# Down products of a bilinear gated unit: seven block products in place of eight, with weight combinations made once

## The chip, the cores and the metric

One core of a Trainium2 chip runs the kernel. The metric is the device time of one execution in microseconds. Nothing in the change or in what is told below involves a second core.

The engines are named as the profile names them: PE is TensorE (PEld its weight loads), DVE is VectorE, ACT is ScalarE, POOL is GpSimd, SP is SyncE, which here only issues transfers.

## The reference

2048 tokens of 640 features pass through a conditioned block of two parts, an S4 convolution and a bilinear gated unit (F = 1536). All is float32.

```
mod = silu(c) @ w_mod                            # six rows of 640: sa, ca, ga, sb, cb, gb
h = layernorm(x) * (1 + ca) + sa
x = x + ga * s4(h)                               # long convolution by FFT, plus a skip
h = layernorm(x) * (1 + cb) + sb
x = x + gb * (((h @ w_gate) * (h @ w_up)) @ w_down)
```

## The kernel before

**Stages.** The first 518 us or so are the modulation, the S4 convolution and the head of the second layernorm; the change leaves them alone. Then comes the gated unit. Its 2048 tokens are taken in two halves, each of two blocks (T = 0 and 1) of 512 tokens; the 1536 hidden features in NF = 12 tiles of 128, the 640 features in NB = 5 tiles of 128. A half has a gate/up loop over the 12 tiles f, and then the down products of its two blocks, one block after the other.

**A product is three matmuls.** Every float32 operand is split into a rounded part `hi` and a rest `lo` (`hilo`, line 1022): ScalarE copies, VectorE subtracts. A product is then hi·hi + lo·hi + hi·lo, three matmuls that add in PSUM (`prod`, line 1055).

**Gate and up.** The two weights and the two token blocks make a 2x2 scheme with seven products in place of eight. For each tile f these are called x_1, x_2, y_1, y_2, y_3, z_1, z_2. In matmuls of 128x512: x_1, y_1 and y_2 have 6, x_2, y_3, z_1 and z_2 have 9, 54 in all. x_1 and x_2 use the plain gate weights (`split_g`); the others use sums of weights (`sums_u` on GpSimd, lines 1036 to 1039; `split_u`) and sums of tokens (`s_sums`, `s_split`). Each product has a PSUM bank of its own out of six that take turns (`pa`, line 1063). The products are put together outside TensorE: `e` is x_1 copied by ScalarE; s6 = y_1 + e; z is z_1 copied by ScalarE; s67 = y_2 + s6; s6 = z + s6; z = z + s67 (GpSimd, line 1412); then the two halves' products a·c (VectorE, line 1423) and s·z (GpSimd, line 1430) are the hidden values. There is one buffer each for s6, z and s67.

**Order.** In each tile the loop calls y_1, z_1, x_1(i+3), parts of `split_u(i+1)`, y_2, `split_g`, `sums_u(i+2)`, x_2(i+3), y_3, z_2, and in the first half `fold(f)`. Engines run their own instructions in the order in which the code issues them.

**Down.** `fold` multiplies w_down by the row gb on GpSimd (line 1507) and writes it to DRAM as `wdg`. `raw` reloads it by SyncE, two tiles at a time, and once for every one of the four token blocks; `d_prep` splits the weights and the hidden values each time. `down` (line 1463) does for each tile 4 token groups x 3 matmuls x 2 column parts of 384 and 256, and adds over all 12 tiles in six banks. `fin` adds the residual and writes the result.

Of the kernel before, what the change touches and what calls it, by code (L numbers as in the profile page):

```python
# [224 lines left out]
def tile_kernel(ctx: ExitStack, tc: tile.TileContext, I, out):  # L225
# [762 lines left out]
    LEFT = {"wga", "wgb", "wur", "xb0", "xb1", "hh1", "hl1", "a5", "a6", "a7", "a8", "a9", "wsgh", "wsgl", "e"}  # L988

    PAIRS = []  # L990
    for h in range(2):
        PAIRS += [("g", h * NF + 2 * p) for p in range(NF // 2)]
        PAIRS += [("d", 2 * h + T, 2 * p) for T in range(2) for p in range(NF // 2)]

    def raw():

        k = PAIRS.pop(0)
        t = mk("wga", [P, 2 * D], F32, 2)
        f = k[-1] % NF
# [25 lines left out]

    def split_g(i):
        WS[i] = mk("wsgh", [P, NB, P], F32R, 4), mk("wsgl", [P, NB, P], F32R, 4)
        hilo(*WS[i], WR.pop(("g", i)))
        if i > 3:
            used(i)  # L1030

# [23 lines left out]
    def prod(ps, ks):  # L1055

        for n, (a, b) in enumerate(((0, 0), (1, 0), (0, 1))):
            for m, (w, k, x, l) in enumerate(ks):
                PE.matmul(ps, w[a][:, k], x[b][:, l], start=n == 0 and m == 0, stop=n == 2 and m == len(ks) - 1)  # L1059

    BANK = [0]

    def pa(j=None):

        if j is None:
            j = BANK[0]
            BANK[0] += 1
        return ps_a.tile([P, 512], F32, name=f"pa{j % 6}")
# [5 lines left out]
    def x_c(i):  # L1074
        V.tensor_tensor(a_tile(i % NF), UX.pop(i), UE[i], op=OP.add)

    def x_1(i):
        UX[i] = pa()
        prod(UX[i], [(WS[i], k, HX[0], k) for k in (0, 1)])
        x_e(i)  # L1080

    def x_2(i, c=True):
        UX[i] = pa()
# [17 lines left out]
    def head_st(tb):  # L1101
        if tb == 1:
            return a_tile(TV0 + NB - 1)[:, : 24 * NB].rearrange("p (i k s) -> p i k s", i=4, k=NB)
        return wp.tile([P, 4, NB, 6], F32, name="st0")
# [547 lines left out]
```

## Time and profile before

| | |
|---|---|
| runs | 1006.97, 1004.3, 1001.61 us; median 1004.3 |
| profiled execution | 1001.29 us; its span 999.2 us; mean granted TensorE clock 0.961 |
| busy, of the span | PE 900.0 us, DVE 762.8, POOL 564.3, ACT 561.9 |
| gated unit, first half | gate/up loop to about 674 us, down to 756 us |
| gated unit, second half | gate/up loop from 761 to 910 us, down to 995 us |

The profile is one execution. The sections of its page give each engine's busy time, groups of equal instructions with their mean length, the chain of work that ended last, and the transfers. A window of the trace gives the same for a stretch of time. An engine's idle time matters only where another engine, or the end, waits for it.

### The profile page before, as it was taken

To read this page: it belongs to the slowest core of one execution; us is meant where nothing else is said; L and a number is where in the kernel's file an instruction comes from. 1 tells how busy PE (TensorE), PEld (TensorE's weight loads), DVE (VectorE), ACT (ScalarE), POOL (GpSimd) and SP (SyncE) were. 2 spreads that over 40 slices of the span, in tenths; PEclk is the share of its full clock that TensorE was granted. 3 is DMA by queue.
4 is the path that set the end of the run, shared out by engine and by line. 5 is a ranking of instruction groups with operands and counts; after the bars stand their busy time and mean duration, and the time that the engine had idled before them with its cause. 6 is when DMAs were issued, how large, how long until landed. Compare 5 with 4: busy or idle time off the path is not lost.

```text
span 999.2 us, 26832 instructions
## 1 busy us (share of the span) xinstructions
PE 900.0 (90%) x11192; PEld 727.2 (73%) x11192; DVE 762.8 (76%) x1399; ACT 561.9 (56%) x1048; POOL 564.3 (56%) x415
## 2 busy tenths in 40 slices
PE   4867898899789689998888999999999999999998
PEld 3565556675576467776555888879998888889998
DVE  8798569889979997975769788777576887768452
ACT  4869989987878979752354323235463422223331
POOL 5978899799789899930032667650112365542000
PEclk9877889999899899999999999999999999999999
DMA  8728754555256454577673442535635232212341
GB/s 265 254 50 301 227 176 135 194 163 167 68 163 202 129 161 120 164 248 214 210 210 123 153 150 87 184 132 159 209 134 202 88 105 80 79 53 59 100 159 53
DMA packets 147817, 153.16 MB, mean 153 GB/s; under 512 B 9200, under 2 KB 125424, under 8 KB 146288
## 3 DMA queue, kind: packets, MB, share of 16 engines
q1 hardware_dynamic: 145968, 148.43, 46.8%
q10 hardware_dynamic: 1728, 3.02, 0.8%
q8 instruction: 88, 1.44, 0.6%
q14 instruction: 33, 0.27, 0.1%
HBM read 110.45 MB, written 40.96 MB: 152 GB/s over the span
## 4 chain that ended last, share of the span: by engine, by line
PE 63%; DVE 16%; ACT 10%; issue 4%; DMA 4%; POOL 2%; SPq 1%; DVEq 0%; ACTq 0%; POOLq 0%
PE pa L1059 26%; PE pa L1463 16%; PE kg L807 2%; DMA xsb<-A_u 2%; PE kg L822 2%; PE psfc L889 2%; ACT L230 1%; PE psfb L889 1%; PE psfa L889 1%; PE psfc L946 1%; PE psfb L946 1%; PE psfa L946 1%; PE psfc L868 1%; ACT trb L230 1%; PE psfa L844 1%
## 5 line engine op out<-in xcount | busy, mean ns | idle before, releaser
L710 POOL TENSOR_TENSOR EQ<-LQ,RH 128x1536 f32<-128x1536 f32 x40 | 124.2, 3105 | 9.9 <-DVE QtB L767 9.7
L230 ACT ACTIVATE z<-pa 128x512 f32<-128x512 f32 x24 | 14.4, 598 | 175.7 <-POOL a L1430 112.1
L1024 DVE TENSOR_TENSOR wsgl<-wga,wsgh 128x640 fp32r<-128x640 f32 x72 | 70.0, 976 | 46.1 <-ACT wsgh L230 46.1
L1412 POOL TENSOR_TENSOR z<-z,s 128x512 f32<-128x512 f32 x24 | 32.1, 1337 | 126.5 <-DVE s L1411 72.0
L230 ACT ACTIVATE wsgh<-wga 128x640 fp32r<-128x640 f32 x72 | 52.5, 732 | 65.1 <-PE pa L1463 47.9
L1024 DVE TENSOR_TENSOR wtl<-tf,wth 128x256 fp32r<-128x256 f32 (+1 forms) x72 | 42.7, 594 | 48.3 <-ACT wth L230 48.3
L1463 PE MATMUL pa<-wsgh,sh 128*128 128x384 f32 (+1 forms) x304 | 69.4, 309 | 0.0
L1463 PE MATMUL pa<-wsgh,sl 128*128 128x384 f32 (+1 forms) x304 | 69.0, 308 | 0.0
L1463 PE MATMUL pa<-wsgl,sh 128*128 128x384 f32 (+1 forms) x304 | 69.0, 308 | 0.0
L710 POOL TENSOR_TENSOR Phb<-LH,DH 128x1536 int32<-128x1536 int32 x20 | 62.3, 3115 | 11.2 <-ACT tra L230 11.2
L710 POOL TENSOR_TENSOR EP<-LP,RH 128x768 f32<-128x768 f32 x40 | 66.1, 1651 | 0.0
L710 POOL TENSOR_TENSOR Pha<-LH,DH 128x1536 int32<-128x1536 int32 (+1 forms) x21 | 62.5, 2974 | 2.2 <-ACT trb L230 1.9
L1036 POOL TENSOR_TENSOR tf<-wur,wgb 128x256 f32<-128x256 f32 x23 | 17.8, 776 | 75.6 <-DVE wtl L1024 50.0
L822 PE MATMUL kg<-QtB,PtB 64*32 64x64 f32 x2560 | 48.7, 229 | 5.4 <-DVE QtB L766 5.3
L822 PEld LDWEIGHTS kg<-QtB,PtB 64*32 64x32 f32 x2560 | 41.6, 114 | 15.4 <-issue 6.5
L1463 PEld LDWEIGHTS pa<-wsgh,sl 128*128 128x128 f32 x304 | 46.4, 187 | 0.0
L1463 PEld LDWEIGHTS pa<-wsgl,sh 128*128 128x128 f32 x304 | 46.3, 187 | 0.0
L1059 PE MATMUL pa<-sh,wtl 128*128 128x512 f32 x144 | 45.0, 394 | 1.4 <-DVE wtl L1024 1.2
L1463 PEld LDWEIGHTS pa<-wsgh,sh 128*128 128x128 f32 x304 | 46.3, 187 | 0.0
L1059 PE MATMUL pa<-sh,wth 128*128 128x512 f32 x144 | 44.9, 393 | 0.5 <-ACT wth L230 0.5
L1059 PE MATMUL pa<-sl,wth 128*128 128x512 f32 x144 | 44.5, 390 | 0.0
L1430 POOL TENSOR_TENSOR a<-s,z 128x512 f32<-128x512 f32 x24 | 38.8, 1618 | 5.4 <-DVE s L1429 5.4
(604 smaller groups left out, 2925.2 us busy)
## 6 DMA issues: line engine op xcount, KB each, us to landing
wga<-wdg SPq DMA_DIRECT2D x24, 640.0 KB, 5.0
wga<-B_w_gate SPq DMA_DIRECT2D x12, 640.0 KB, 5.9
wgb<-B_w_gate SPq DMA_DIRECT2D x24, 320.0 KB, 3.4
wur<-B_w_up SPq DMA_DIRECT2D x24, 320.0 KB, 4.0
xb<-x2d SPq DMA_DIRECT2D x6, 1280.0 KB, 5.7
TVb<-WD SPq DMA_DIRECT2D x22, 256.0 KB, 3.6
t_tw<-w_mod SPq DMA_DIRECT2D x3, 1600.0 KB, 8.5
t_ti<-w_mod SPq DMA_DIRECT2D x3, 1600.0 KB, 7.9
```

The source lines that it names most:

```text
L230: return S.activation(o, i, f, **kw)
L710: G.tensor_tensor(o.rearrange("p x (h l) -> p x h l", l=8), lo.unsqueeze(2).to_broadcast([P, rows, nh, 8]), hi.rearrange("p h x -> p x h") ...
L807: PE.matmul(kg[j * 32 : j * 32 + 32, dd, :], PtA[:, c, dl * 4 + j, :], QtA[:, c, dl * 4 + j, :], start=dd == 0 and c == 0, stop=False, til ...
L822: PE.matmul(kg[j * 32 : j * 32 + 32, dd, :], PtB[lo : lo + 64, c, r, :], QtB[lo : lo + 64, c, r, :], start=False, stop=dd == 7 and c == 1, ...
L889: PE.matmul(r[c][par * 64 : par * 64 + 64, i, :], t_tw[:, k0 + k, c, :], src[:, k, :], start=True, stop=True, tile_position=(0, par * 64))
L946: PE.matmul(r[par][:, i], t_ti[lo : lo + 64, qd * 4 + i, c, :], x[lo : lo + 64, c, i, :], start=c == 0, stop=c == 1, tile_position=(lo, 0))
L1024: V.tensor_tensor(lo, v, hi, op=OP.subtract)
L1036: E.tensor_tensor(t[:, 0:2], u[:, 0:2], g[:, 0:2], op=OP.subtract)
L1059: PE.matmul(ps, w[a][:, k], x[b][:, l], start=n == 0 and m == 0, stop=n == 2 and m == len(ks) - 1)
L1412: G.tensor_tensor(ZT[i], ZT[i], S67[i], op=OP.add)
L1430: G.tensor_tensor(a_tile(NF + i % NF), c, ZT.pop(i), op=OP.mult)
L1463: PE.matmul(ACC[tb][t][c], x[:, ts], w[:, cs], start=st, stop=f == NF - 1 and n == 2 and (c == 0 or t % 2 == 1))
```

## The change

**Down.** A half's down product is seen as a 2x2 block product: two token blocks, two halves of the hidden features (NH = 6 tiles each), two halves of 320 output columns. Seven block products j = 0 to 6 give it. `down(half, m)` is tile c of product j, m = 6j + c, with 12 matmuls of 320 columns. The sums over j stay in PSUM in two sets of four banks, "A" and "C"; `post` adds them to the residual after each product. The sums of hidden values are made by `d_sum` on GpSimd, from the end of the gate/up loop to m = 14.

**Weights.** In the first half's loop `f_load` fetches four tiles of w_down, `f_sums` multiplies them by gb and forms the combinations on GpSimd, and `f_put` splits the seven of them and writes both parts to DRAM (`wdc`). The three rounds are placed by a table over slots, three slots a tile. `w_load` brings 640 KB of these split weights by a transfer that GpSimd issues and that casts to the matmul's type, one for every two m. The split gate weights are kept in DRAM too (`wsd`), and the second half reloads them in the same way.

**Gate and up.** x_1, y_1, y_2 and y_3 of a tile now add in one bank, z_1 and z_2 in another. s67 is gone; s6 is a copy by ScalarE (for the first two tiles, whose x_1 comes earlier, still an addition by VectorE, with z + e and the last product on GpSimd). The product a·c moves from VectorE to GpSimd, the other from GpSimd to VectorE.

```
     def split_g(i):
-        WS[i] = mk("wsgh", [P, NB, P], F32R, 4), mk("wsgl", [P, NB, P], F32R, 4)
+        t = wsg()
+        WS[i] = tuple(t[:, j].rearrange("p (k m) -> p k m", k=NB) for j in range(2))
+        if i >= NF:
+            G.dma_start(t, wsd[:, i - NF])
+            return
         hilo(*WS[i], WR.pop(("g", i)))
...
     def x_1(i):
-        UX[i] = pa()
-        prod(UX[i], [(WS[i], k, HX[0], k) for k in (0, 1)])
+        UX[i] = UA[i] = pa(i % 4)
+        prod(UX[i], [(WS[i], k, HX[0], k) for k in (0, 1)], last=False)
         x_e(i)
...
     def y_1(i):
-        ps = pa()
-        prod(ps, [(WT[i], 2 + k, HX[2], 2 + k) for k in range(2)])
+        if i < 2:
+            UA[i] = pa(i)
+        prod(UA[i], [(WT[i], 2 + k, HX[2], 2 + k) for k in range(2)], i < 2, False)
         S6[i] = tmp("s6")
-        V.tensor_tensor(S6[i], ps, UE[i], op=OP.add)
+        if i < 2:
+            V.tensor_tensor(S6[i], UA[i], UE[i], op=OP.add)
+        else:
+            act(S6[i], UA[i])
 
     def z_1(i):
...
+        if i < 2:
+            G.tensor_tensor(ZT[i], ZT[i], UE[i], op=OP.add)
 
     def y_2(i):
-        ps = pa()
-        prod(ps, [(WT[i], 4 + k, HX[2], 4 + k) for k in range(2)])
-        S67[i] = tmp("s67")
-        V.tensor_tensor(S67[i], ps, S6[i], op=OP.add)
-        V.tensor_tensor(S6[i], ZT[i], S6[i], op=OP.add)
-        G.tensor_tensor(ZT[i], ZT[i], S67[i], op=OP.add)
+        prod(UA[i], [(WT[i], 4 + k, HX[2], 4 + k) for k in range(2)], False, False)
+        V.tensor_tensor(ZT[i], UA[i], ZT[i], op=OP.add)
 
     def z_2(i):
...
-        V.tensor_tensor(a, a, c, op=OP.mult)
+        G.tensor_tensor(a, a, c, op=OP.mult)
 
     def y_3(i):
...
+        if i < 2:
+            V.tensor_tensor(UE[i], UA.pop(i), UE[i], op=OP.add)
+            G.tensor_tensor(h, UE.pop(i), ZT.pop(i), op=OP.mult)
+        else:
+            V.tensor_tensor(h, UA.pop(i), ZT.pop(i), op=OP.mult)
...
+    def d_prep(m):
+        j, c = divmod(m, NH)
+        v = S1[c] if j == 3 else AT[(0, NH, 0, 0, NF, NH, NF + NH)[j] + c]
+        AH[m] = d_pair(m)
+        hilo(*AH[m], v)
...
+    def d_sum(j, c, E=G):
+        a, b = AT[c], AT[NF + c]
+        if j == 0:
...
+            E.tensor_tensor(S1[c], b, AT[NF + NH + c], op=OP.add)
+            E.tensor_tensor(b, a, b, op=OP.subtract)
+        elif j == 1:
+            E.tensor_tensor(a, S1[c], a, op=OP.subtract)
+        else:
+            E.tensor_tensor(AT[NH + c], AT[NH + c], a, op=OP.subtract)
+
+    def w_load(q):
+        WD[q] = wsg()
+        G.dma_start(WD[q], wdc[:, q // 3, q % 3])
+
+    def down(half, m, last=False):
...
+        w = [WD[m // 2][:, l, c % 2 * DC : c % 2 * DC + DC] for l in range(2)]
+        for t in range(4) if not last else (last - 1,):
+            for n, (a, b) in enumerate(((0, 0), (1, 0), (0, 1))):
+                PE.matmul(ps[t][:, :DC], AH[m][a][:, t * P : t * P + P], w[b], ...)
...
+    def post(half, j, ts=range(4), E=None):
...
+        for t in ts:
+            V.tensor_tensor(x[:, t], ps[t][:, :DC], x[:, t], op=OP.add)
...
+    def f_sums():
+        for k in range(4):
+            G.tensor_tensor(FT["f"][:, k], FT["f"][:, k], gbr, op=OP.mult)
...
+        G.tensor_tensor(t[:, 1], b22, b12, op=OP.subtract)
+        G.tensor_tensor(b12, b12, b11, op=OP.subtract)
+        G.tensor_tensor(t[:, 0], b22, b12, op=OP.subtract)
+        G.tensor_tensor(t[:, 2], b21, t[:, 0], op=OP.subtract)
+
+    def f_put(r, j, n):
...
+        act(k(hi), v)
+        V.tensor_tensor(v.bitcast(F32R), v, k(hi), op=OP.subtract)
+        SY.dma_start(wdc[:, j, r, 0], hi.bitcast(F32))
+        SY.dma_start(k(wdc[:, j, r, 1]), v)
...
+    FOLD[2] = [(f_sums,)]
+    FOLD[10], FOLD[13] = [(f_load, 1)], [(f_sums,)]
+    FOLD[21], FOLD[24] = [(f_load, 2)], [(f_sums,)]
+    for r, b in enumerate((4, 15, 26)):
+        for j in range(7):
+            FOLD[b + j] = [(f_put, r, j, r + j), *FOLD[b + j]]
...
         for f in range(NF):
             i = i0 + f
+            late = 0 < f <= NF - AHEAD
             y_1(i)
-            z_1(i)
-            late = 0 < f <= NF - AHEAD
             if late:
                 x_1(i + AHEAD - 1)
+            z_1(i)
+            fold(half, 3 * f)
...
-            y_3(i)
-            z_2(i)
-            if half == 0:
-                fold(f)
+            z_2(i)
+            fold(half, 3 * f + 1)
+            y_3(i)
+            fold(half, 3 * f + 2)
...
+        for m in range(7 * NH):
...
+            if todo and m > 0:
+                d_sum(*todo.pop(0))
+            if m % 2 == 0 and m and m // 2 + 3 < 21:
+                w_load(m // 2 + 3)
...
+                down(half, m)
+            if c == 0 and j:
+                post(half, j - 1)
```

How the change moves instructions is seen on three places. The first is GpSimd in the first half's loop, from the z of tile 0 to the z of tile 1. In the rows the name and line stand first, then what is written, what is read, and the shape; `tf` are sums of gate and up weights, `a_...` hidden values, `xb_...` the tiles of w_down. Before:

```order
L1412 TENSOR_TENSOR z<-z,s_7816 128x512
L1036 TENSOR_TENSOR tf<-wur,wgb 128x256
L1037 TENSOR_TENSOR tf<-wur,tf 128x256
L1038 TENSOR_TENSOR tf<-wur 128x256
L1039 TENSOR_TENSOR tf<-wgb,tf 128x256
L1430 TENSOR_TENSOR a_7852<-s_7816,z 128x512
L1412 TENSOR_TENSOR z<-z,s_7911 128x512
```

The same place after, from line 1437 of tile 0, which is a·c, on to the z of tile 1 (line 1423):

```order
L1437 TENSOR_TENSOR a_7630<-a_7630,s_7791 128x512
L1444 TENSOR_TENSOR a_7862<-e,z 128x512
L1546 TENSOR_TENSOR xb_7780<-xb_7780,gbr 128x640 x4
L1550 TENSOR_TENSOR xb_7781<-xb_7780 128x640
L1551 TENSOR_TENSOR xb_7780<-xb_7780 128x2x320
L1552 TENSOR_TENSOR xb_7781<-xb_7780 128x640
L1553 TENSOR_TENSOR xb_7781<-xb_7780,xb_7781 128x640
L1423 TENSOR_TENSOR z<-z,e 128x512
```

The four sums `tf` still stand ahead of line 1437; the eight operations of `f_sums` are new between the two tiles.

The second place is TensorE in tile 0 of the first half: y_1, z_1 and y_2 before, each writing a bank of its own (`pa_7782`, `pa_7791`, `pa_7809`).

```order
L1059 MATMUL pa_7782<-sh,wth 128x512 x2
L1059 MATMUL pa_7782<-sh,wtl 128x512 x2
L1059 MATMUL pa_7782<-sl,wth 128x512 x2
L1059 MATMUL pa_7791<-sh,wth 128x512 x2
L1059 MATMUL pa_7791<-hh_7624,wsuh 128x512
L1059 MATMUL pa_7791<-sh,wtl 128x512 x2
L1059 MATMUL pa_7791<-hh_7624,wsul 128x512
L1059 MATMUL pa_7791<-sl,wth 128x512 x2
L1059 MATMUL pa_7791<-hl_7625,wsuh 128x512
L1059 MATMUL pa_7809<-sh,wth 128x512 x2
```

After, in the same place:

```order
L1063 MATMUL pa_7784<-sh,wth 128x512 x2
L1063 MATMUL pa_7784<-sh,wtl 128x512 x2
L1063 MATMUL pa_7784<-sl,wth 128x512 x2
L1063 MATMUL pa_7793<-sh,wth 128x512 x2
L1063 MATMUL pa_7793<-hh_7620,wsuh 128x512
L1063 MATMUL pa_7793<-sh,wtl 128x512 x2
L1063 MATMUL pa_7793<-hh_7620,wsul 128x512
L1063 MATMUL pa_7793<-sl,wth 128x512 x2
L1063 MATMUL pa_7793<-hl_7621,wsuh 128x512
L1063 MATMUL pa_7784<-sh,wth 128x512 x2
```

The matmuls keep their order; y_2 now writes y_1's bank again.

The third place is GpSimd at the start of the first half's down products. Before, it had the end of the loop and weight sums of the next half:

```order
L1412 TENSOR_TENSOR z<-z,s_8915 128x512
L1430 TENSOR_TENSOR a_7647<-s_8915,z 128x512
L1036 TENSOR_TENSOR tf<-wur,wgb 128x256
L1037 TENSOR_TENSOR tf<-wur,tf 128x256
L1038 TENSOR_TENSOR tf<-wur 128x256
```

After, it has these (line 1489 is `w_load`, lines 1480 to 1483 are `d_sum`):

```order
L1489 DMA wsg<-wdc 128x1280 x2
L1480 TENSOR_TENSOR hh_8826<-a_8308,a_7642 128x512
L1481 TENSOR_TENSOR a_8308<-a_7634,a_8308 128x512
L1480 TENSOR_TENSOR hst<-a_8416,a_7643 128x512
L1481 TENSOR_TENSOR a_8416<-a_8060,a_8416 128x512
L1489 DMA wsg<-wdc 128x1280
L1483 TENSOR_TENSOR a_7630<-hh_8826,a_7630 128x512
L1483 TENSOR_TENSOR a_7631<-hh_8826,a_7631 128x512
L1489 DMA wsg<-wdc 128x1280
L1483 TENSOR_TENSOR a_7632<-hh_8826,a_7632 128x512
L1483 TENSOR_TENSOR a_7633<-hh_8826,a_7633 128x512
L1489 DMA wsg<-wdc 128x1280
```

Between the loads stand the sums of hidden values, two for each load, up to m = 14; the loads then follow one another with nothing between them.

288 lines of the change are left out of this document (155 added, 133 removed).

## The prediction, made before the result was known

> **What bounds the kernel now.** I read the page first, for who is busy; then the busy time in windows cut at the stages of the gated unit; then the chain of waits over that stretch; then single timelines at the places that the change touches. The page:
>
> ```profile
> span 999.2 us, 26832 instructions
> PE 900.0 (90%) x11192; PEld 727.2 (73%) x11192; DVE 762.8 (76%) x1399; ACT 561.9 (56%) x1048; POOL 564.3 (56%) x415
> ```
>
> The execution took 1001.29 us, so 2.1 us lie around the span. It is 3.0 us below the median of the runs, 1004.3; I make the sum on 1001.3 and add 3 at the end. Everything before about 518 us is left alone. The rest in windows (us, then busy time of each engine, the granted clock, the DMA share and rate):
>
> ```profile
> 520.00:545.00 25.00, 22.23 (x91) 15.15 (x90) 22.32 (x40) 14.93 (x30) 1.35 (x1) 1.00 0.37 124
> 545.00:664.00 119.00, 118.89 (x519) 96.87 (x518) 95.20 (x133) 33.17 (x77) 82.61 (x73) 1.00 0.42 138
> 664.00:675.00 11.00, 9.46 (x52) 8.13 (x51) 8.97 (x13) 4.78 (x8) 3.19 (x3) 1.00 0.49 179
> 675.00:756.00 81.00, 80.96 (x562) 80.72 (x561) 56.51 (x129) 43.24 (x70) 12.06 (x11) 1.00 0.50 163
> 756.00:761.00 5.00, 3.79 (x27) 3.53 (x25) 4.36 (x5) 2.97 (x5) 3.01 (x2) 1.00 0.00 0
> 761.00:910.00 149.00, 148.66 (x648) 121.45 (x649) 110.18 (x166) 46.08 (x102) 66.83 (x63) 1.00 0.31 98
> 910.00:995.00 85.00, 84.98 (x578) 84.57 (x576) 40.39 (x62) 27.03 (x44) 1.64 (x2) 1.00 0.31 97
> 995.00:1000.00 5.00, 0.00 (x0) 0.00 (x0) 1.22 (x3) 0.00 (x0) 0.00 (x0) 0.92 0.55 198
> ```
>
> In order these are: the start of the first half's gate/up loop, the loop, its end, the first half's down products, the turn to the second half, its gate/up, its down products, the last writes. TensorE is busy for 99.9% of the long windows at a granted clock of 1.00. Only 2.8 us are idle at the start, 1.5 us at 664:675 and 1.2 us at 756:761. So fewer matmul columns are worth their full time, and any new wait of TensorE costs its full time: there is nothing left to hide behind. The chain says the same, and prices a matmul:
>
> ```profile
> 674.50 41.92 PE pa L1463 x284
> 761.34 149.04 PE pa L1059 x648
> 910.38 84.62 PE pa L1463 x576
> 995.02 0.42 DVE xb L1478
> ```
>
> Line 1463 is the down product: 84.62/576 = 146.9 ns for a mean width of 320 columns. Line 1059 is gate/up: 149.04/648 = 230 ns for 512 columns.
>
> **The gain.** Down had 4 token blocks x 12 f x 24 = 1152 matmuls of 384 and 256 columns, 169.2 us. Seven block products of 6 f-tiles for eight leave 2 halves x 42 x 12 = 1008 matmuls of 320 columns. At the same 146.9 ns a pair of uneven ones becomes two even ones: 148.1 us. Gain 21.1 us. Gate/up keeps its 1296 matmuls. All else can only take from this.
>
> **A: the start of the first loop, +15.** The products x_1, y_1, y_2, y_3 of a tile now add into one bank, and tiles 0 and 1 have VectorE read that bank between them. The matmul rows are the start of y_2(0), of y_1(1) and of x_1(4), by the order of instructions; the last row is VectorE's read of y_1(0). A row begins with its start and length in us.
>
> ```profile
> 532.32 0.62 PE L1059 MATMUL pa<-sh,wth 128*128 128x512 f32 x2
> 540.14 0.74 PE L1059 MATMUL pa<-sh,wth 128*128 128x512 f32 x2 [0.51 <-ACT wth L230]
> 545.56 0.63 PE L1059 MATMUL pa<-hh,wsgh 128*128 128x512 f32 x2
> 540.23 0.69 DVE L1398 TENSOR_TENSOR s<-pa,e 128x512 f32<-128x512 f32 x1
> ```
>
> (a) Before, y_2(0) ran 8 us ahead of that read, in a bank of its own. Now it waits for the read, which ends at 540.9; what stands ahead of the read on VectorE has not changed. Then y_2, z_2 and y_3 are 24 matmuls, 5.5 us, so y_1(1) starts at 546.4 and not 540.14: +6.3. Before, the 15 matmuls from 540.14 to 545.56 were 3.45 us of work in 5.4, held by split weights that came late; at 546.4 these are there, so 1.9 us are won back: +4.4.
>
> (b) Before, nothing but short sums stood on GpSimd between tile 0 and tile 1. Now the first f_sums stands there, 8 operations of 128x640, ahead of z+e(1). The first row is h(0); the groups below it have busy us and mean ns of one, then the idle time before them:
>
> ```profile
> 548.80 1.75 POOL L1430 TENSOR_TENSOR a<-s,z 128x512 f32<-128x512 f32 x1
> L1507 POOL TENSOR_TENSOR xb<-xb,gbr 128x640 f32<-128x640 f32 x12 | 18.8, 1588 | 0.0
> L1374 POOL TENSOR_TENSOR a<-a,a 128x512 f32<-128x512 f32 x2 | 2.6, 1302 | 14.5 <-ACT a L230 14.5
> ```
>
> The product h(0) ended at 550.6 and should end near 551 again (its add on VectorE comes at about 547, and GpSimd has the four sums and a new a*c product ahead). Then 8 x 1.588 = 12.7 us, z+e(1) 1.3 us: 565. VectorE's add of y_2(1) needs z+e(1), and y_3(1) must not overwrite the shared bank before that add: 566. TensorE reaches y_3(1) after 45 matmuls from 546.4, at 556.8. So +9 us of idle TensorE. (c) VectorE's list, held in that add, is then behind, and x_1(5) needs what it splits: +2. Sum 15.4, taken as 15. Ends: 9, if f_sums overlaps with less (8 operations at the 1.3 us row save 2.3, and the 4.4 may partly be won back because GpSimd's loss counts from a later tile start), and 18.
>
> **B: f_sums 2 and 3 and f_put, +9.** Two more f_sums stand in tiles 4 and 8.
>
> ```profile
> 556.41 0.75 POOL L1036 TENSOR_TENSOR tf<-wur,wgb 128x256 f32<-128x256 f32 x1 [1.10 <-DVE wtl L1024]
> 557.23 1.21 POOL L1037 TENSOR_TENSOR tf<-wur,tf 128x256 f32<-128x256 f32 x1
> 558.40 0.74 POOL L1038 TENSOR_TENSOR tf<-wur 128x256 f32<-128x256 f32 x1
> 559.11 0.73 POOL L1039 TENSOR_TENSOR tf<-wgb,tf 128x256 f32<-128x256 f32 x1
> L230 ACT ACTIVATE wsgh<-wga 128x640 fp32r<-128x640 f32 x72 | 52.5, 732 | 65.1 <-PE pa L1463 47.9
> L1024 DVE TENSOR_TENSOR wsgl<-wga,wsgh 128x640 fp32r<-128x640 f32 x68 | 67.0, 986 | 46.1 <-ACT wsgh L230 46.1
> xb<-B_w_down SPq DMA_DIRECT2D x2, 1280.0 KB, 9.0
> ```
>
> In steady state a tile is 54 x 0.230 = 12.4 us of TensorE; GpSimd has 1.6 us of product and 3.4 us of sums in it, so 12.7 us of f_sums leave it 5 us late. What it is late with is a*c, which frees the one s6 buffer; ScalarE's next copy of y_1 into s6 waits, and the bank with it. With x_1, z_1 and the rest between I take 2.5 us for the second, and 5 for the third (its 1.3 MB of weights are asked for one tile, 12.4 us, earlier, and behind the last f_put, whose buffer they take; their landing alone is 9.0 us; and the last tiles have no x products to cover). f_put adds 21 ScalarE and 21 VectorE passes of 640 (0.73 and 0.99 us) to the loop; VectorE loses two adds a tile and a product, so the net is small, but they stand ahead of adds that free banks: +1.5. Bounds 0 (all absorbed in GpSimd's 7 us of slack a tile) and 17.
>
> **C: the down stages, +10.** No weight is split there any more, but GpSimd must, for every two block steps (24 matmuls, 3.53 us), form two sums and issue one casting transfer of 640 KB:
>
> ```profile
> L1024 DVE TENSOR_TENSOR wsul<-wur,wsuh 128x384 fp32r<-128x384 f32 x24 | 37.4, 1558 | 0.0
> L1024 DVE TENSOR_TENSOR wtl<-tf,wth 128x512 fp32r<-128x512 f32 x24 | 16.3, 680 | 0.0
> wga<-wdg SPq DMA_DIRECT2D x24, 640.0 KB, 5.0
> 533.93 0.37 SPq L1018 DMA_DIRECT2D wgb<-B_w_gate  x1
> ```
>
> The two sums are 2 x 1.302 = 2.6 us. VectorE's subtractions, two of 0.68 us in the same 3.53 us, read SBUF twice, and the first row shows what such an instruction suffers beside GpSimd: 384 columns take 1558 ns where 512 take 680. I charge GpSimd 1.2 us for them. Issuing a transfer from GpSimd is in no row of this trace; the nearest row is an issue of SyncE, 0.37 us, and I take 0.5. Together 4.3 us against 3.53, until the sums run out after the fourteenth step: 0.8 us lost for each of seven pairs, with the loads (5.0 us to landing) issued behind the sums, the third needed 7 us into the stage and landing at about 8.5. +5 a half. Ends 1.5 (no loss from VectorE) and 9 (2 us of issue).
>
> The Trainium skill, "SBUF — State Buffer", section "Who interferes with whom", says that a VectorE instruction with two SBUF inputs contends with a GpSimd instruction that reads SBUF, because the second input comes through the shared read interface. The 1558 against 680 ns agree. Without that rule C would be 1.5 us a half, so the sum would be 7 us lower. The Trainium skill, "DMA: Bandwidth & Descriptors", section "Anatomy of one DMA — SWDGE (gpsimd) path", fits 2.0 us plus bytes/436e3 to such a transfer: an estimate of 3.5 us for 640 KB, which would take about 1 us off C in each half. No run here shows it.
>
> **Nothing.** The turn to the second half, its loop (no f_sums, gate weights reloaded ready split) and the tail: 0, within 1. They add as many waits as they remove: the 1.2 us at 756:761 stays, the last writes still follow the last matmul by 4 us.
>
> **Sum.** 1001.3 - 21.1 + 15 + 9 + 10 = 1014.2, and 3 to the median: 1017 us. Ends: 1001.3 - 21.1 + 9 + 0 + 3 = 992 (995) and + 18 + 17 + 18 = 1033 (1036).
>
> **Rivals.** *R1, faster, 997 us.* GpSimd catches up after tile 1. For it: in 545:664 it is idle 31%, and it loses a multiplication a tile. Then A 10, B 1, C 3: 994, and 997 at the median. It decides when the waits stay under 16 us; against it, (a) and (b) rest on order alone and make 13 by themselves. Chance 0.18. *R2, no change, 1006 us.* A 15, but the bursts are mostly absorbed, B 4, C 4: 1003. Chance 0.16. *R3, much slower, 1069 us.* The casting transfer itself paces the down stage: the nearest row, 5.0 us for 640 KB, is more than 3.53; were they one after another, 42 x 5.0 = 210 us against 148: +62 in place of C's 10, 1066. Against it: the 5.0 us are a latency, and the DMA share is 0.50 in 675:756. It decides as soon as one load costs more than 3.53 us of the queue. Chance 0.09. My forecast, 1017 (own range 1009 to 1036), keeps 0.57.
>
> **Chances.** A measurement of this kernel can tell 0.5%, 5 us. Faster by more: R1, 0.18. Within: R2, 0.16. Slower: 0.57 + 0.09 = 0.66. The range leaves out most of R3 (0.07) and the lower half of R1 (0.09): 995 to 1040.
>
> **What would show it.** In the changed kernel's trace: y_1(1) starts near 546; TensorE idles for some 9 us between 556 and 566 with line 1423 on GpSimd late behind lines 1546 to 1553; smaller holes in tiles 4 and 8 to 9; holes before matmuls of line 1502 released by the transfers of wsg, in the first 14 steps of each half; the matmuls themselves at 147 ns. Wrong if a matmul of 320 columns costs other than 147 ns, if the first loop takes no longer than before, or if the transfers hold TensorE to the end of a down stage.

## The result, and the profile after

The changed kernel takes 1042.4 us (median of four runs, 1038.4 to 1043.6) against 1004.2 us before: a ratio of 1.037, 95% interval 1.033 to 1.041. The forecast was slower, at 1017 us; the measured time lies above the range (995 to 1040). The profiled execution took 1043.28 us with a span of 1041.5 us.

The page of the changed kernel, its span, busy times and transfers from GpSimd:

```profile
span 1041.5 us, 26772 instructions
PE 899.6 (86%) x11048; PEld 721.1 (69%) x11048; DVE 728.8 (70%) x1352; ACT 571.3 (55%) x1069; POOL 647.5 (62%) x509
wsg<-wdc POOLq DMA_DIRECT2D x42, 640.0 KB, 4.4
```

TensorE has 144 matmuls less and is no less busy. To see where, I divided both traces at the same events: the first y_1 matmul, and the first and last down matmul of each half. The columns are the window, its length, busy time of PE, PEld, DVE, ACT and POOL, the granted clock, DMA share and rate. First before, in the order first loop, first down stage, turn and second loop, second down stage:

```profile
527.80:668.40 140.60, 137.72 (x590) 109.45 (x590) 115.44 (x166) 45.24 (x102) 84.59 (x74) 1.00 0.43 142
668.40:759.80 91.40, 89.81 (x617) 88.75 (x615) 64.83 (x138) 48.75 (x80) 17.30 (x15) 1.00 0.46 153
759.80:910.20 150.40, 148.86 (x648) 121.63 (x649) 111.38 (x167) 46.27 (x102) 67.36 (x64) 1.00 0.31 97
910.20:995.00 84.80, 84.78 (x577) 84.39 (x575) 40.39 (x62) 26.83 (x44) 1.44 (x2) 1.00 0.31 98
```

Then the changed kernel:

```profile
533.70:711.20 177.50, 145.73 (x588) 115.09 (x589) 101.83 (x155) 64.70 (x133) 110.16 (x88) 0.91 0.63 211
711.20:801.10 89.90, 81.73 (x539) 80.70 (x538) 69.66 (x142) 37.84 (x66) 43.18 (x49) 0.96 0.77 237
801.10:954.50 153.40, 150.49 (x656) 123.19 (x655) 68.90 (x121) 51.03 (x110) 64.88 (x74) 0.99 0.36 103
954.50:1037.90 83.40, 76.77 (x505) 73.93 (x503) 58.49 (x71) 22.45 (x38) 35.34 (x38) 1.00 0.65 196
```

The first loop is 37 us longer, with 32 us of idle TensorE and a clock of 0.91. The down stages are 1.5 us shorter each, not 10.5. The turn costs 3 us. The lead up to the first y_1, 533.7 against 527.8, does the same work in both; over the kernels below that leave it alone it came out between 526 and 534, so kernels are compared by their stages.

Two places show what happens. In the first down stage, VectorE (first six rows) and GpSimd (last three), each with start and length:

```profile
712.02 1.30 DVE L1013 TENSOR_TENSOR hl<-a,hl 128x512 fp32r<-128x512 f32 x1
713.25 5.80 DVE L1013 TENSOR_TENSOR sl<-a,sh 128x512 fp32r<-128x512 f32 x3
724.30 4.30 DVE L1013 TENSOR_TENSOR sl<-a,sh 128x512 fp32r<-128x512 f32 x2
731.21 0.17 DVE L276 TENSOR_SCALAR hr<-mv 128x4 f32<-128x4 f32 x1
731.87 2.75 DVE L279 TENSOR_TENSOR hr<-hr 128x4 f32<-128x4 f32 x1
734.66 0.16 DVE L280 TENSOR_TENSOR hr<-hr,hr 128x4 f32<-128x4 f32 x1
728.58 1.30 POOL L1483 TENSOR_TENSOR a<-hh,a 128x512 f32<-128x512 f32 x1
729.83 1.29 POOL L1483 TENSOR_TENSOR a<-hst,a 128x512 f32<-128x512 f32 x1
732.09 2.50 POOL L1485 TENSOR_TENSOR a<-a,a 128x512 f32<-128x512 f32 x2
```

Subtractions that took 0.7 us before take 1.3 to 2.2 us. The plainest row is line 279: an operation on 128x4 values, with two inputs, took 2.75 us, and ended when the two GpSimd sums beside it had ended (732.09 + 2.50); its neighbours of the same size, with GpSimd at rest, took 0.16. GpSimd's own sums took 1.3 to 1.5 us in the mean of each line. VectorE, the third busy time in the window of the stage's start, is full:

```profile
711.00:740.00 29.00, 20.83 (x115) 19.80 (x114) 27.41 (x49) 8.51 (x15) 22.89 (x21) 0.88 0.66 215
```

In the first loop it is different: VectorE is busy for 101.8 of 177.5 us, less than before (115.4). There it stands still, behind results of GpSimd. GpSimd (first four rows) has f_sums between h(0) and z+e(1), and TensorE's y_3(1) waits 8.3 us for VectorE, which waits for z+e(1). In the second round VectorE does nothing for 9.4 us, since the next operation in its list is a split of f_put on a tile with which f_sums is not yet done (last row):

```profile
557.88 1.29 POOL L1444 TENSOR_TENSOR a<-e,z 128x512 f32<-128x512 f32 x1
559.13 6.35 POOL L1546 TENSOR_TENSOR xb<-xb,gbr 128x640 f32<-128x640 f32 x4
570.40 1.53 POOL L1553 TENSOR_TENSOR xb<-xb,xb 128x640 f32<-128x640 f32 x1
571.88 1.26 POOL L1423 TENSOR_TENSOR z<-z,e 128x512 f32<-128x512 f32 x1
573.93 1.22 PE L1063 MATMUL pa<-hh,wth 128*128 128x512 f32 x2 [8.26 <-DVE z L1427]
628.26 0.83 DVE L1561 TENSOR_TENSOR xb<-xb,hst 128x640 fp32r<-128x640 f32 x1 [9.41 <-POOL xb L1551]
```

### The profile page after: what moved, and what is told of

The parts are those of the page before. It is cut to its first block, busy times and chain, and to the rows that moved or that the text cites. A ratio compares the mean times of both kernels' runs of the same rounds, so it can differ in the third digit from the quotient of the medians.

```text
span 1041.5 us, 26772 instructions
## 1 busy us (share of the span) xinstructions
PE 899.6 (86%) x11048; PEld 721.1 (69%) x11048; DVE 728.8 (70%) x1352; ACT 571.3 (55%) x1069; POOL 647.5 (62%) x509
## 4 chain that ended last, share of the span: by engine, by line
PE 44%; DVE 17%; POOL 14%; ACT 11%; issue 8%; DMA 5%; SPq 1%; DVEq 0%; POOLq 0%; ACTq 0%
PE pa L1063 14%; PE pa L1502 5%; PE psg L1063 4%; DVE sl L1013 2%; PE kg L822 2%; PE kg L807 2%; POOL xb L1546 2%; DMA wdc<-xb 2%; PE psfb L889 1%; PE psfc L889 1%; PE psg L1502 1%; ACT L230 1%; PE psfc L946 1%; ACT trb L230 1%; POOL Pha L710 1%
## 5 line engine op out<-in xcount | busy, mean ns | idle before, releaser
L230 ACT ACTIVATE s<-pa 128x512 f32<-128x512 f32 x22 | 13.2, 599 | 146.2 <-POOL a L1437 85.2
L1502 PE MATMUL pa<-wsg,sh 128*128 128x320 f32 x312 | 75.9, 316 | 5.1 <-DMA wsg<-wdc 3.5
L710 POOL TENSOR_TENSOR Phb<-LH,DH 128x1536 int32<-128x1536 int32 x20 | 62.3, 3117 | 16.8 <-ACT tra L230 16.8
L1013 DVE TENSOR_TENSOR sl<-a,sh 128x512 fp32r<-128x512 f32 x60 | 66.6, 1156 | 2.5 <-ACT sh L230 2.4
L1489 POOL DMA_DIRECT2D wsg<-wdc x42 | 23.5, 559 | 68.6 <-PE psg L1502 34.7
L1502 PEld LDWEIGHTS pa<-wsg,sh 128*128 128x128 f32 x312 | 55.2, 194 | 5.8 <-issue 3.7
L1502 PE MATMUL pa<-wsg,sl 128*128 128x320 f32 x156 | 50.0, 321 | 8.5 <-DVE sl L1013 8.5
L230 ACT ACTIVATE sh<-a 128x512 fp32r<-128x512 f32 x60 | 34.6, 622 | 38.8 <-DVE sl L1013 17.5
L1063 PE MATMUL pa<-hh,wsg 128*128 128x512 f32 x166 | 44.4, 396 | 5.5 <-DVE a L1446 5.5
L1517 DVE TENSOR_TENSOR wga<-pa,wga 128x320 f32<-128x320 f32 x44 | 19.4, 484 | 31.7 <-PE pa L1502 31.7
L1063 PEld LDWEIGHTS pa<-sh,wth 128*128 128x128 f32 x126 | 24.3, 198 | 24.2 <-ACT s L230 9.9
L1063 PE MATMUL pa<-sh,wtl 128*128 128x512 f32 x126 | 40.8, 407 | 0.1
```

The source lines that it names most:

```text
L230: return S.activation(o, i, f, **kw)
L710: G.tensor_tensor(o.rearrange("p x (h l) -> p x h l", l=8), lo.unsqueeze(2).to_broadcast([P, rows, nh, 8]), hi.rearrange("p h x -> p x h") ...
L1013: V.tensor_tensor(lo, v, hi, op=OP.subtract)
L1063: PE.matmul(ps, w[a][:, k], x[b][:, l], start=first and n == 0 and m == 0, stop=n == 2 and m == len(ks) - 1, skip_group_check=True)
L1489: G.dma_start(WD[q], wdc[:, q // 3, q % 3])
L1502: PE.matmul(ps[t][:, :DC], AH[m][a][:, t * P : t * P + P], w[b], start=c == 0 and n == 0 and j in (0, 1, 3), stop=c == NH - 1 and n == 2, ...
```

## The experiments

The theory after the result: GpSimd's operations that read SBUF hold VectorE's operations with two SBUF inputs, and GpSimd's blocks stand ahead of what VectorE and TensorE need next; so TensorE waits in the first loop and at the beginnings of the down stages. These are two causes, and the runs below tell where each of them counts. The rivals: the casting transfers come late; VectorE simply has too much to do; a low clock behind each wait makes the loss.

All stages, in us, divided as above (time is one run, but for the kernel before, the changed one and e11, where it is the profiled one; next to the experiments the kernel before took 999.5 to 1003.2 us):

| | time | lead | first loop | first down | turn, second loop | second down |
|---|---|---|---|---|---|---|
| before | 1001.3 | 527.8 | 140.5 | 91.4 | 150.4 | 84.8 |
| changed | 1043.3 | 533.7 | 177.5 | 89.9 | 153.4 | 83.4 |
| e1_puts_later | 1041.6 | 529.7 | 177.9 | 89.9 | 155.0 | 83.6 |
| e2_warm | 1040.3 | 530.6 | 177.4 | 89.5 | 153.5 | 83.9 |
| e3_no_dsum | 1019.8 | 528.7 | 178.2 | 80.1 | 152.1 | 75.2 |
| e4_sums_ahead | 1039.4 | 528.8 | 176.6 | 91.4 | 153.8 | 83.1 |
| e5_dsum_dve | 1027.2 | 527.0 | 177.6 | 87.4 | 154.1 | 75.6 |
| e6_dsum_spread | 1029.3 | 525.9 | 177.4 | 88.2 | 153.8 | 78.6 |
| e7_fsums_dve | 1021.3 | 527.9 | 160.8 | 90.4 | 153.6 | 83.2 |
| e8_fsums_spread | 1040.0 | 531.2 | 175.8 | 90.1 | 153.5 | 84.0 |
| e9_comb | 1009.3 | 530.4 | 164.0 | 78.7 | 154.1 | 76.7 |
| e10_comb_pre | 1003.7 | 526.1 | 162.9 | 78.7 | 154.1 | 76.5 |
| e11_gap | 991.5 | 524.5 | 153.4 | 81.7 | 150.6 | 75.8 |
| e12_no_fsums | 986.9 | 524.1 | 145.0 | 85.4 | 150.5 | 76.5 |

Stages whose code two kernels share agree within 2 us (the first down stage is 89.5 in e2 and 91.4 in e4), so a difference of less than 2 us in a stage is not a reading.

The first loop by tiles, each counted from its first y_1 matmul to that of the next tile. The blocks of the three rounds of f_sums stand in the changed kernel at the end of tile 0 and within tiles 4 and 8, so that each of the last three columns holds one round:

| | tile 0 | 1 to 4 | 5 to 8 | 9 to 11 |
|---|---|---|---|---|
| before | 12.3 | 51.7 | 49.6 | 26.9 |
| changed | 21.5 | 62.8 | 57.3 | 36.0 |
| e1_puts_later | 21.7 | 60.4 | 55.0 | 40.8 |
| e4_sums_ahead | 30.9 | 53.0 | 57.6 | 35.3 |
| e7_fsums_dve | 22.1 | 55.3 | 53.0 | 30.3 |
| e8_fsums_spread | 22.4 | 57.6 | 56.6 | 39.1 |
| e11_gap | 18.6 | 53.8 | 49.7 | 31.3 |
| e12_no_fsums | 17.3 | 50.9 | 49.8 | 27.0 |

**e1: the splits of the combinations later.**

```
-    FOLD[10], FOLD[13] = [(f_load, 1)], [(f_sums,)]
-    FOLD[21], FOLD[24] = [(f_load, 2)], [(f_sums,)]
-    for r, b in enumerate((4, 15, 26)):
+    FOLD[11], FOLD[14] = [(f_load, 1)], [(f_sums,)]
+    FOLD[23], FOLD[26] = [(f_load, 2)], [(f_sums,)]
+    for r, bs in enumerate((range(5, 12), range(17, 24), (29, 30, 30, 31, 31, 32, 32))):
```

> Rounds 2 and 3 of the weight combinations are placed so that the first f_put of a round stands three slots behind f_sums (about 12.4 us) and not two (8.3 us); the last seven stand two to a slot. Theory 1 (f_put waits on VectorE for f_sums, and VectorE's list waits behind it: 9.4 us idle ahead of line 1561 at 618:628): the hole of VectorE shrinks to under 5 us, and tile 5 to 6 of the first loop, 18.5 us in the changed kernel, falls to about 14; the first half's loop gets 3 to 7 us shorter. Rival (GpSimd's 12.7 us are themselves too many for the tile, through a*c and the one s6 buffer): the length of the loop stays within 2 us.

The loop takes 177.9 us, as the rival said, but not for the rival's reason alone. In the second round VectorE no longer stands still for 9.4 us ahead of line 1561, and the tiles of the first two rounds are 2.4 and 2.3 us shorter: about that much the early splits had cost there. In tiles 9 to 11, where this run also puts the third round's splits two to a slot, the loop is 4.8 us longer, and this hides the gain. What stays of the second round, 5.4 us over the kernel before, is the rival's: from copy to copy of z, tile 5 to 6 is 17.8 us and not 14. Behind f_sums, which ran from 612.6 to 626.0, come the sums of the next weights and only then a*c, and ScalarE waits 10.8 us for it; VectorE's subtractions beside f_sums take 1.9 and 2.1 us:

```profile
620.71 1.92 DVE L1013 TENSOR_TENSOR wsul<-wur,wsuh 128x384 fp32r<-128x384 f32 x1
622.56 2.05 DVE L1013 TENSOR_TENSOR wtl<-tf,wth 128x512 fp32r<-128x512 f32 x1
629.35 1.86 POOL L1437 TENSOR_TENSOR a<-a,s 128x512 f32<-128x512 f32 x1
631.25 0.60 ACT L230 ACTIVATE s<-pa 128x512 f32<-128x512 f32 x1 [10.77 <-POOL a L1437]
```

**e2: the clock.** 32 unused matmuls ahead of y_3(1):

```
+        if i == 1:
+            ps = pg()
+            for _ in range(32):
+                PE.matmul(ps, WU[i][0][:, 3], HX[1][0][:, 2], start=True, stop=True)
```

> 32 matmuls of 512 columns, whose sums nobody reads, stand ahead of y_3(1), where TensorE waits 8.3 us for z+e(1). They are 7.4 us of work at full clock and lie in that wait. Theory (the granted clock is halved for some 5 us after a wait of over 3 us): the granted clock stays 1.00 from 566 to 580 us, and the 45 matmuls from y_3(1) on take 2 to 2.7 us less; the kernel gets faster by 2 to 3 us although TensorE does more. Rival (the low clock there has nothing to do with the wait): the clock falls to 0.5 all the same, and the tile takes no less.

The changed kernel's wait and what follows it, in windows of 4 us (the clock is the third number from the end):

```profile
566.00:570.00 4.00, 0.00 (x0) 0.00 (x0) 0.00 (x0) 0.26 (x1) 3.84 (x3) 0.84 0.00 0
570.00:574.00 4.00, 0.07 (x1) 0.07 (x1) 0.82 (x2) 0.00 (x0) 3.07 (x3) 0.50 0.00 0
574.00:578.00 4.00, 4.00 (x10) 3.13 (x11) 4.00 (x8) 0.00 (x0) 2.57 (x3) 0.50 0.25 95
578.00:582.00 4.00, 4.00 (x17) 3.23 (x16) 1.64 (x3) 0.48 (x1) 4.00 (x4) 0.88 0.95 270
```

And e2, the same place some 3 us earlier, then its next wait of TensorE:

```profile
570.00:574.00 4.00, 2.98 (x13) 2.46 (x14) 3.72 (x7) 0.00 (x0) 1.71 (x3) 1.00 0.00 0
574.00:578.00 4.00, 2.15 (x10) 1.51 (x9) 3.17 (x5) 0.00 (x0) 4.00 (x4) 1.00 0.81 242
576.58 1.17 PE L1063 MATMUL pa<-hh,wsg 128*128 128x512 f32 x4 [1.85 <-DVE e L1447]
```

The clock is halved by the wait, and filling the wait keeps it: 10 matmuls in 4 us there, 13 in 3 us here. By the shares above it fell 3.1 us after the last matmul had ended (565.7) and came back 5.1 us after the next one had begun (573.9). The Trainium skill, "TensorE: Matmul & The Clock Gate", section "Part 1: The HAM clock gate", has half the clock after an idle window of about 3.4 us, and the full clock after about as long at work. The trace agrees in kind; the return took longer here. But the loop gained 0.1 us, not 2 to 3: the faster matmuls met a new wait of 1.85 us for VectorE, which was behind in any case. So the low clock is shown, and in this place it costs next to nothing. Over the whole loop the matmuls are busy for 8 us more than before (145.7 against 137.7); the other waits were not filled, so what the low clock costs behind them is not shown.

**e3: no sums of hidden values.** The bodies of `d_sum` are taken out.

> Left out: the sums of hidden values (d_sum); the split takes plain hidden values in their place, so products two to five are of other values. Instructions of TensorE, loads, splits and posts are unchanged. Theory 1 (GpSimd's sums hold up VectorE's subtractions with two SBUF inputs): the subtractions of line 1013 on hidden values fall from 1156 ns in the mean to about 700, and the down stages from 90.7 and 83.4 us to about 80 and 75 us, 18 us less in all. Theory 2 (the casting transfers are late): no subtraction matters, TensorE still waits for wsg, and the stages stay over 88 and 82 us.

Both stages fell as theory 1 said, by 9.8 and 8.1 us, with the same transfers, so theory 2 is out. The loads do come sooner here, with no sums ahead of them on GpSimd, but this is not what counts: TensorE's waits for wsg were 3.5 us in the first stage and 0.5 in the second in the changed kernel, and are 2.3 and 0.9 in e3, while its waits for splits of hidden values, 4.6 and 6.0 us, are gone. The subtractions of hidden values, in the groups by line (busy us, mean ns | idle before), first before, then changed, then e3:

```profile
L1024 DVE TENSOR_TENSOR sl<-a,sh 128x512 fp32r<-128x512 f32 x50 | 35.5, 719 | 4.1 <-ACT sh L230 4.1
L1013 DVE TENSOR_TENSOR sl<-a,sh 128x512 fp32r<-128x512 f32 x60 | 66.6, 1156 | 2.5 <-ACT sh L230 2.4
L1013 DVE TENSOR_TENSOR sl<-a,sh 128x512 fp32r<-128x512 f32 x70 | 45.2, 698 | 3.5 <-ACT sh L230 3.4
```

**e5: the same sums on VectorE** (`def d_sum(j, c, E=V)`). **e6: on GpSimd, but later:**

```
-    SUMS = [(0, 4), (0, 5)] + [(j, c) for j in (1, 2) for c in range(NH)]
+    SUMS = {1: (1, 0), 3: (1, 1), 5: (1, 2), 6: (0, 4), 8: (1, 3), 9: (0, 5), 11: (1, 4), 12: (1, 5)}
+    SUMS.update({14 + 2 * c: (2, c) for c in range(NH)})
```

> The sums of hidden values (d_sum) are made by VectorE in the same places, not by GpSimd. Theory 1 (the loss of the down stages is GpSimd's hold on VectorE's second read): VectorE gets 24 more instructions of 0.7 us a half, but its subtractions fall from 1156 to about 700 ns; the down stages shrink from 89.9 and 83.3 us to 80 to 85 and 75 to 80. Rival (VectorE is simply out of time at the start of the stage, 27.4 us busy in 29): it has still more to do there, and the stages stay or get longer.

> GpSimd keeps the sums of hidden values, but makes them as late as their readers allow: up to m = 24 in place of m = 14, about one operation for each 2 us. Theory 1 with the lock only where both meet: fewer meetings in the first 14 steps, where VectorE has no slack: down stages some 4 to 7 us shorter each. Rival (any sum on GpSimd costs VectorE the same whenever it comes): the stages stay within 2 us.

e5 gives VectorE all of GpSimd's sums, and its subtractions take 702 ns again:

```profile
L1013 DVE TENSOR_TENSOR sl<-a,sh 128x512 fp32r<-128x512 f32 x60 | 40.1, 702 | 2.5 <-ACT sh L230 2.5
L1481 DVE TENSOR_TENSOR a<-a,a 128x512 f32<-128x512 f32 x12 | 9.3, 773 | 0.4
L1481 POOL TENSOR_TENSOR a<-a,a 128x512 f32<-128x512 f32 x12 | 17.9, 1492 | 0.9
```

(The last row is the changed kernel's.) The second down stage is at 75.6 us, e3's 75.2 without any sums: there almost the whole loss was the meeting of the two engines. The first is at 87.4, short of e3's 80.1 and of what was expected: there VectorE also has the statistics of the next tokens in the first steps, and the rival is half right. e9 moves these, among other changes, and the stage comes to 78.7. e6 lies between: the sums cost less when they come later, in the second half as was expected (4.8 us); in the first the 1.7 us are no reading, as its rival had it.

**e4, e7, e8: where the weight combinations are formed.** e4 puts the first f_sums ahead of the loop, with an earlier load; e7 gives all to VectorE in three slots, with the splits where they were; e8 leaves them on GpSimd in five slots, and its splits then stand two to a slot.

```
e4:  -    FOLD[2] = [(f_sums,)]
     ...
     +            f_sums()                       # after the loads ahead of the loop
...
e7:  +        for d, (l_, h_) in enumerate(((0, 3), (3, 6), (6, 8))):
     +            FOLD[b + d] = [(f_sums, l_, h_, V), *FOLD[b + d]]
...
e8:  +        for d, (l_, h_) in enumerate(((0, 2), (2, 4), (4, 6), (6, 7), (7, 8))):
     +            FOLD[b + d] = [(f_sums, l_, h_, G), *FOLD[b + d]]
```

> The first load of w_down and the row gb are asked for ahead of the token sums, and the first f_sums stands ahead of the loop, where GpSimd was idle for 25 us. Theory 1 (f_sums between the first two tiles costs its 12.7 us and the low clock behind it): tile 1 to 2, 23.3 us in the changed kernel, falls to 12 to 14, the loop is 9 to 13 us shorter. Rival (the first tiles are bound by VectorE's list and by late weights): under 4 us, or the time comes back at z+e(0), if the load lands only after 545 us.

> The weight combinations of w_down are formed by VectorE, three, three and two operations in the slot of f_sums and the two after it; GpSimd has none of it. Theory 1 (GpSimd's 12.7 us blocks hold z+e and a*c, and VectorE's subtractions beside them): tiles 1 to 2 and 5 to 6, 23.3 and 18.5 us in the changed kernel, fall to 13 to 15, and the first loop from 177.6 to 155 to 162 us. Rival (VectorE, with 7 to 8 us more a round, is the next bound): the loop shrinks by under 8 us.

> f_sums stays on GpSimd but its eight operations stand two, two, two, one, one in five slots; the splits that follow stand two to a slot. Theory (the block of 12.7 us is what hurts, as it stands ahead of z+e and a*c): the first loop falls by 10 us or more. Rival (each operation holds VectorE's subtractions wherever it stands, and GpSimd has too little time in a tile): it falls by under 5 us.

e4's tile 1 to 2 did fall, from 23.3 to 12.4 us, but the loop by 1 us only: tile 0 is 9.4 us longer. The load had landed by 526 us, so it was not late as the rival had it. GpSimd's block (first row) now runs beside VectorE's token sums and splits (second row: two subtractions in 4.0 us, which take 1.3 in the changed kernel), and TensorE waits for those, 7.8 us in one place:

```profile
526.14 7.50 POOL L1546 TENSOR_TENSOR xb<-xb,gbr 128x640 f32<-128x640 f32 x4 [11.28 <-DMA xb<-B_w_down]
528.23 4.00 DVE L1013 TENSOR_TENSOR sl<-a,sh 128x512 fp32r<-128x512 f32 x2
543.85 1.19 PE L1063 MATMUL pa<-sh,wth 128*128 128x512 f32 x2 [7.80 <-DVE a L1086]
```

e7 took 16.8 us off the loop, as expected: what costs is that GpSimd does the work. VectorE is busier by as much as the loop is shorter (119.0 us in 160.8, against 101.8 in 177.5). e8 took off 1.8, which is no reading. Here too a second effect hides a first: tile 1 is at 12.4 us, 22.8 in the changed kernel, and tiles 1 to 4 together are 5.2 us shorter, but tiles 9 to 11 are 3.1 longer. ScalarE waits for the transfers that empty the buffers of the crowded splits, up to 8.8 us (the longest such wait in the changed kernel's loop is 2.9):

```profile
588.37 0.74 ACT L230 ACTIVATE hst<-xb 128x640 fp32r<-128x640 f32 x1 [8.81 <-DMA wdc<-hst]
```

So e8 does not tell what spreading the block alone would do; that stays open.

**e9 and e10: together.** e9 is e5 and e7 with the combinations from tile 1's end on and the statistics from m = 15 on. e10 also moves two reads of VectorE ahead of the first loop:

```
             s_one(4)
+            x_c(2)
             split_u(0, "b")
             for k in range(2):
                 s_split(k, 3)
-            x_c(2)
             split_u(0, "c")
+            y_1(0)
...
```

> Three edits together: the sums of hidden values and the weight combinations on VectorE (the latter from tile 1's end on, three rounds of three, three and two operations), and the statistics of the next tokens moved from m = 1 to 11 to m = 15 to 25. Theory 1: the first loop is 177.6 - 16.8 (as measured for VectorE alone) - 3 to 5 (no combinations in the first two tiles) = 155 to 158 us, the first down stage 80 to 83 and the second 75.6 us; the kernel takes 1006 to 1012 us. Rival (VectorE's time is the next bound, so that the two do not add up): loop over 160 or first down stage over 86 us, 1015 us or more.

> As e9_comb, and ahead of the loop VectorE reads x_2(2)'s bank before the up weights are split, and y_1(0)'s bank as soon as the weights are split, not after the token sums. Theory (a) of the prediction (y_2(0) waits, in y_1(0)'s bank, for VectorE's list): the 3.3 and 4.9 us waits ahead of z_1(0) and y_2(0) go, and with them the half clock; the loop is 5 to 8 us shorter than e9_comb. Rival (the first tile needs the whole list of VectorE anyway, since z_2(0) and y_3(0) read its other results): under 2 us.

e9's time is as expected and its parts are not: the down stages are 78.7 and 76.7, the loop 164.0, more than e7's 160.8 and over the 160 that the rival named. VectorE has four operations of combinations and splits between TensorE's end of y_3 and the product that frees y_3's bank, and x_1 of a later tile waits:

```profile
576.92 1.00 DVE L1551 TENSOR_TENSOR xb<-xb 128x640 f32<-128x640 f32 x1
580.38 1.88 DVE L1559 TENSOR_TENSOR xb<-xb,hst 128x640 fp32r<-128x640 f32 x1
582.18 0.68 DVE L1446 TENSOR_TENSOR a<-pa,z 128x512 f32<-128x512 f32 x1
583.01 1.45 PE L1063 MATMUL pa<-hh,wsg 128*128 128x512 f32 x4 [4.22 <-DVE a L1446]
```

e10's first tile, from copy to copy of z, fell from 16.7 to 12.7 us, but the loop by 1.1: the rival held for the loop as a whole. The kernel's time is 5.6 us below e9's, 4.3 of it in the lead; leads differ by as much between kernels that leave the lead alone.

**e11: behind the last product of a tile.**

```
+    for r, (a_, b_, p_) in enumerate(((2, 5, (6, 7, 8, 9, 10, 11, 12)), (15, 17, (18, 19, 20, 21, 22, 23, 24)), (27, 29, (30, 31, 32, 33, 34, 35, 35)))):
...
+        FOLD[a_] = [(f_sums, 0, 4, V), *FOLD[a_]]
+        FOLD[b_] = [(f_sums, 4, 8, V), *FOLD[b_]]
...
-        s4 = a_tile(21) if k else tmp(TMP[1])
+        s4 = a_tile(21 if k else 23)
...
             for k in range(2):
                 s_split(k, 3)
+            y_1(i0)
             for k in range(2):
                 s_split(k, 4)
-            s_five()
+            s_five(G, a_tile(22))
```

> As e10_comb_pre, and: the combinations are formed four at a time right behind a tile's last product, where VectorE otherwise waits some 5 us for split weights, and not three at a time ahead of y_3's product; the first load of w_down is asked for ahead of the loop; two token sums get buffers of their own, so that the copies of y_1 and z_1 of a half's first tile do not wait for them, and the second half's y_1 copy stands ahead of its last token splits. Theory 1 (what is left in the first loop is VectorE's list ahead of y_3's product, and in the turn the one s6 buffer): the waits of 4.0 and 2.0 us ahead of the x_1 of tiles 7 and 8 and of 2.9 us at the turn go, the first loop takes 150 to 156 us, turn and second loop 150 to 152, the kernel 990 to 996 us, faster than before by 0.8 to 1.4%. Rival (VectorE is out of time in the loop wherever the operations stand): loop over 160, kernel about 1000 us.

994.6 us (median of four runs) against 1002.7 before on the same chip: a ratio of 0.993, interval 0.991 to 0.996: 0.7% less time than the kernel before, a small gain whose interval is clear of 1. Against the profiled execution before, the four stages are 5.6 us shorter and the lead 3.3; what of the lead comes of the new order and what is chance is not shown. The loop is at 153.4, turn and second loop at 150.6, both as expected (the second row is the second down stage):

```profile
524.50:677.90 153.40, 142.11 (x588) 113.11 (x589) 117.62 (x183) 61.57 (x128) 63.33 (x58) 0.97 0.67 221
910.20:986.00 75.80, 74.58 (x505) 73.82 (x503) 49.06 (x88) 22.13 (x38) 10.33 (x20) 1.00 0.72 215
```

**e12: e11 without the combinations.**

> e11_gap with the 24 combinations of w_down left out (a clear of the tile stands for them; the splits write what they find), so its weights are of other values. It prices what is left of forming them in the first loop, 153.4 us in e11_gap against 140.5 us in the kernel before. Theory (VectorE's list, 24 operations of about 1.1 us, is what is left): the loop takes 144 to 148 us. Rival (the shared banks, the splits and their transfers are what is left): it stays over 150 us.

145.0 us, as the theory said: forming them on VectorE still costs 8.4 us of the loop. The first down stage is 3.7 us longer, where TensorE waits 4.5 us for splits and 2.2 in e11, so over both stages the combinations cost 4.7 us. Of the 12.9 us by which e11's loop is longer than that before, 4.5 are left without the combinations, and the table by tiles tells where: tile 0 is 5.0 us longer than before, and the other tiles together take no more than before, although the splits of f_put and their transfers stand in them.

## Why the prediction was wrong

- **The gain** was right. Line 1502's matmuls run at 3.52 us for 24, 146.7 ns, and with no sums the second down stage is 75.2 us against 73.9 of matmuls.
- **A, +15, was 18.6**, just over its upper end of 18. The order was seen rightly. By y_1(1), tile 0 had lost 9.2 us where (a) has 6.3: the wait at y_2(0) came as worked out, and another at z_1(0), for VectorE's read of x_2(2)'s bank, was not foreseen (rows below). Tiles 1 and 2 lost 9.4 us more, where the rest of A makes 9.1; the wait at y_3(1) was 8.3 us where (b) has 9, and behind it TensorE ran at half clock.
- **B, +9, was 18.4**, over its upper end of 17; here the price of a block of f_sums failed. The second was taken at 2.5 us and cost 7.7 (tiles 5 to 8), the third at 5 and cost 9.1; tile 3, which has splits of f_put and no block, lost 1.7. The wait for a*c and the one s6 buffer had been named. What failed is the step from GpSimd's lateness to TensorE's loss. The second block took 13.4 us (618.8 to 632.2), and the a*c behind it came at 637.5, 20.0 us after the one before and so 7.6 us more than a tile's 12.4: late by 7.6 and not by 5. The prediction let x_1 and z_1 cover half of that, and they covered nothing. Two waits follow the block: VectorE, whose list has f_put next, stands still for 9.4 us, and, when this is taken away in e1, ScalarE waits 10.8 us for a*c. Moving the work to VectorE recovered 16.8 us of A and B together.
- **C, +10, was 18**, its upper end. Here a cost was charged to the wrong engine. The row was seen (384 columns in 1558 ns, 512 in 680) and used the wrong way round: the charge of 1.2 us was put on GpSimd, whose sums took 1.3 to 1.5 us, and not on VectorE, whose subtractions went from 719 to 1156 ns. In the first 29 us of the stage VectorE was busy for 27.4. e3 and e5 show it.
- **Nothing at the turn, within 1**, was 3: one buffer, s6, was shared with the token sums, and y_2 waited 2.9 us for it (last row below). e11's buffers and order took it away.
- **The sum and the range.** With these terms the sum is 1001.3 - 21.1 + 18.6 + 18.4 + 18 + 3 = 1038, and 3 to the median: 1041 us, against 1042.4 measured. The range did add up the upper ends of A, B and C, to 1036, and ended at 1040. It failed because all three came out at or above these ends, and the turn above its 1. That the direction came out right is no luck, since (a) and (b) were worked out from order; it is the sizes that failed, and for two causes: in the loop the longest waits are for what stands behind GpSimd's blocks, in the down stages it is GpSimd's hold on VectorE.
- **The rivals.** R1 and R2 are out by the time. R3 is out: a casting transfer of 640 KB was 0.56 us of GpSimd and 4.4 us to landing, but they overlap, since where no sums are left they are issued every 3.5 us, and TensorE's waits for them sum to 4 us.

The two waits of TensorE in the changed kernel's first tile, and the one at the turn:

```profile
539.02 1.19 PE L1063 MATMUL pa<-sh,wth 128*128 128x512 f32 x2 [3.31 <-DVE a L1086]
547.83 1.19 PE L1063 MATMUL pa<-sh,wth 128*128 128x512 f32 x2 [4.63 <-DVE s L1413]
821.94 1.22 PE L1063 MATMUL pa<-sh,wth 128*128 128x512 f32 x2 [2.91 <-ACT s L230]
```

Without e10's reads ahead of the loop the first two stay; with them tile 0 is 3.4 us shorter by TensorE (22.1 in e9, 18.6 in e10), and later tiles lose 2.4 of it again.

The rule of the Trainium skill cited from "SBUF — State Buffer", section "Who interferes with whom", held: a VectorE instruction with two SBUF inputs contends with a GpSimd instruction that reads SBUF. The traces add who pays here: VectorE, with 437 ns more for a subtraction in the mean, while GpSimd's sums keep 1.3 to 1.5 us. For the casting transfer, the estimate from the Trainium skill, "DMA: Bandwidth & Descriptors", section "Anatomy of one DMA — SWDGE (gpsimd) path", was 3.5 us; the median to landing was 4.4.

Open: what a spread block on GpSimd would cost with its splits one to a slot, and how much of the loop's loss is the low clock behind the waits. The 4.5 us that e11's loop keeps without the combinations lie in tile 0, ahead of the first split of f_put. There e12's TensorE waits 1.1 us at y_2(0) for VectorE's read and 2.3 us at z_2(0) for ScalarE's copy of the banks that these products now share, and part of it runs at half clock; no run gives tile 0 its separate banks back.

## What to carry to other kernels

When work is given to GpSimd because it is idle, look at what VectorE does in the same microseconds: here its operations with two SBUF inputs waited for GpSimd's, so that 1.3 us of GpSimd could cost VectorE as much, and 0.7 us on VectorE itself was cheaper. Put such work where VectorE waits for something else, and behind, not ahead of, the operation that frees a PSUM bank. When an engine gets a block of work that is longer than its idle time in a tile, count all of what is left over as lost until a row shows what covers it. And where a row shows an operation made longer by a neighbour, charge the engine whose row it is.

## What the runs showed of the hardware

- An operation of 128x4 values with two inputs took 2.75 us on VectorE beside two GpSimd sums and ended with the second, and took 0.16 us without them: in this place it was held for more than one whole instruction of GpSimd.
- The granted clock fell to 0.50 within a wait of TensorE of 8.3 us, 3.1 us after its start, and came back 5.1 us after the matmuls had begun again; with unused matmuls in the wait it stayed at 1.00, and the loop gained 0.1 us.
- GpSimd's issue of a casting transfer of 640 KB took 0.56 us of it, and the data were there 4.4 us after (median of 42), at DMA shares of 0.77 and 0.65 in the two down stages.
